# One transfer for the last tile of values, and three pieces of wo instead of four, in a decode attention kernel

## The chip, the cores and the metric

The kernel runs on one core of a Trainium2 chip. The metric is the time of one execution on the device in microseconds (us). Before the change the median of three runs is 190.05 us (189.97 to 190.06).

The core's engines work side by side, each through its own list of instructions in order, and wait for each other by semaphores: TensorE (PE; its weight loads are shown as PEld), VectorE (DVE), ScalarE (ACT), GpSimd (POOL) and SyncE (SP), which here only issues transfers (SPq).

## The reference

One token passes through an attention block with a cache of 4096 positions and through a small two-layer network, and a gate mixes the two. All inputs are bf16, with 32 heads of 128, a model width of 512, and a hidden width of 1376.

```
g = sigmoid((x * gate_w).sum(-1))
q = (x @ wq) per head                       # 32 heads, one query row each
p = softmax(q . k_cache * 128**-0.5)        # over 4096 positions
a = (p . v_cache, heads side by side) @ wo  # (1, 4096) @ (4096, 512)
b = relu(x @ w1 + b1)**2 @ w2 + b2
out = g * a + (1 - g) * b
```

The keys and the values are 32 MB each, wq and wo 4 MB each, w1 and w2 some 2.8 MB together: 78 MB are read for one row of 512 results.

## The kernel before, in words

**Tiles.** The 32 heads are taken four at a time in NQ = 8 tiles. A tile of keys, or of values, is 128 partitions of 32 KB (4 MB): 32 partitions for each head, 128 positions in each partition. Three buffers hold keys (Kt) and two hold values (Vt). The last two tiles of values go into key buffers that have come free (`VT(i)`).

**Order on the engines.** For each tile GpSimd multiplies a part of the keys with the query (L312), VectorE another part (L671) and adds both up (L686, L680), while TensorE transposes the rest (L424) and multiplies it (L438). Then come the maximum (L448, L452), the exponentials on ScalarE (L358), and the sum over the values on TensorE, `pv` (L469): 32 matmuls for a tile, one for each group of four positions, that run in turn in four column strips of the array (the target rows `r = 32 * (y % 4)` of pO). A copy brings pO to pvf, and `extract` (L478, eight matmuls) puts the tile's heads into place in pX.

**The transfers.** SP issues all large loads in one queue, in an order written out by hand (L276 to L293): keys and values in turn, each as soon as its buffer is free, then wo into the first value buffer. The last value tile goes in two transfers (L273, L274): VG = 24 of its 32 groups, then the other eight, each with a semaphore of its own (`s_vl[1]`, `s_vl[2]`). wo, 32 rows of 128 KB (one row per head, 128 partitions by 512 columns), goes in four pieces, whose bounds stand in `TS` (L292).

**The tail on TensorE**, from L590 on: the last but one tile's values and extraction, four fillers (`busy(4)`, L568: matmuls of 512 columns whose result nobody reads), `den()` (the denominators, L485), the last values in two calls of `pv`, three fillers, `extract`, two fillers, `regroup` (L536, which turns the 32 heads' results into columns), three fillers, and then the rows of wo, piece by piece. VectorE lies between these steps: L730 copies pO, L733 divides, L735 copies the regrouped columns.

**Rows of wo.** `attn_rows(c)` waits for piece c. The first WW = 20 rows take one matmul of 512 columns each into pO (L546), in the four strips in turn. The others take four matmuls of 128 columns each, straight into the result in pX (L552). When row 19 is done, VectorE copies pO (L737), and `wide_rows` (L561, eight instructions) adds the copy into pX. After the last row VectorE adds the network's part (L740), and SP sends the result out (L295).

In the kernel before, piece 0 holds rows 0 to 15 and is followed by four fillers; piece 1 holds rows 16 to 23, so the end of the wide rows and the beginning of the narrow ones; before piece 2 (rows 24 to 29) stand two fillers, `wide_rows` and one filler; piece 3 holds rows 30 and 31.

Of the kernel before, what the change touches and what calls it, by code (L numbers as in the profile page):

```python
# [5 lines left out]
def bass_gated_mix__gqa_block_cached__dense_activation_squared_relu__decode_kernel(  # L6
# [22 lines left out]
    NQ = NH // 4  # L29
# [29 lines left out]
    NG = NB // 4  # L59
# [7 lines left out]
    BIG = 3.0e38  # L67


    TS = [0, 16, 24, 30, 32]  # L70
    NW = len(TS) - 1
    WW = 20

    VG = 24


    k_p = A_k_cache.rearrange("a h (q b) d -> (a h q) (b d)", b=NB)
    v_p = A_v_cache.rearrange("a h (q b) d -> (a h q) (b d)", b=NB)
# [7 lines left out]
    with ctx:  # L86
# [6 lines left out]
        def sem(name):  # L93
            return ctx.enter_context(nc.semaphore(name))
# [73 lines left out]
        def VT(i):  # L168
            return Vt[:, i % NV, :] if i < NQ - 2 else Kt[:, (i - 1) % NK, :]
# [21 lines left out]
        s_bb = sem("s_bb")  # L191
        s_k = [sem(f"s_k{i}") for i in range(NK)]
        s_v = [sem(f"s_v{i}") for i in range(NV)]
        s_vl = [sem(f"s_vl{i}") for i in range(3)]
        s_id = sem("s_id")
        s_ho = sem("s_ho")
        s_xc = sem("s_xc")
# [46 lines left out]
        def on(engine):  # L244
            return lambda part: part(engine)

        @on(nc.sync)
        def _(eng):
            def load_k(i):
                if i >= NK:  # L250
                    eng.wait_ge(s_t, CB[i - NK + 1])
                    eng.wait_ge(s_mu, XP * (i - NK + 1))
                    eng.wait_ge(s_pm, GP * (i - NK + 1))
                if i == 2:
                    eng.wait_ge(s_ml, 1)
                eng.dma_start(Kt[:, i % NK, :], k_p[i * 128:(i + 1) * 128, :]).then_inc(s_k[i % NK], 16)

            def load_v(i):
                if i == 1:
                    eng.wait_ge(s_qr, NQ)  # L260
                    eng.wait_ge(s_h, 2)
                if i < NQ - 2:
                    if i >= NV:
                        eng.wait_ge(s_pv, i - NV + 1)
                    eng.dma_start(VT(i), v_p[i * 128:(i + 1) * 128, :]).then_inc(s_v[i % NV], 16)
                    return
                eng.wait_ge(s_t, CB[i])
                eng.wait_ge(s_mu, XP * i)
                eng.wait_ge(s_pm, GP * i)  # L269
                if i == NQ - 2:  # L270
                    eng.dma_start(VT(i), v_p[i * 128:(i + 1) * 128, :]).then_inc(s_vl[0], 16)
                else:
                    for u, a, b in ((1, 0, VG * 512), (2, VG * 512, NG * 512)):  # L273
                        eng.dma_start(VT(i)[:, a:b], v_p[i * 128:(i + 1) * 128, a:b]).then_inc(s_vl[u], 16)  # L274

            load_k(0)  # L276
            eng.dma_start(w1_sb, w1_v).then_inc(s_w1, 16)
            eng.dma_start(w2a, w2_v).then_inc(s_w2, 16)
            eng.dma_start(w2b, B_w2[F0:F1, :]).then_inc(s_w2, 16)
            for r in range(4):  # L280
                eng.dma_start(WX[r:QX:4, :], w2_x[r:QX:4, :]).then_inc(s_w2, 16)
            load_k(1)
            load_v(0)
            load_k(2)
            for i in range(NQ):
                if i >= 1:
                    load_v(i)
                if i + LAG < NQ:
                    load_k(i + LAG)
            eng.wait_ge(s_pv, NQ - 3)  # L290
            for c in range(NW):
                eng.dma_start(WO[:, TS[c] * DM:TS[c + 1] * DM], wo_v[:, TS[c] * DM:TS[c + 1] * DM])\  # L292
                   .then_inc(s_wo[c], 16)  # L293
            eng.wait_ge(s_fin, 1)
            eng.dma_start(out[0, 0, :].rearrange("(j p) -> j p", p=128), b2w[0:128:32, :]).then_inc(s_out, 16)  # L295
            eng.wait_ge(s_out, 16)
# [89 lines left out]
        def _(eng):  # L386
# [69 lines left out]
            def pv(i, a, b):  # L456
                if a == 0:
                    eng.wait_ge(s_e, 4 * (i + 1))
                    if i < NQ - 2:
                        eng.wait_ge(s_v[i % NV], 16 * (i // NV + 1))  # L460
                    else:
                        eng.wait_ge(s_vl[i - (NQ - 2)], 16)
                    if i >= 1:
                        eng.wait_ge(s_pc, i)
                if a == VG and i == NQ - 1:
                    eng.wait_ge(s_vl[2], 16)
                for y in range(a, b):
                    r = 32 * (y % 4)
                    mm = eng.matmul(pO[r:r + 16, :], E[:, i % NE, 4 * y:4 * y + 4, :],  # L469
                                    VT(i)[:, y * 512:(y + 1) * 512], start=(y < 4), stop=(y >= NG - 4))  # L470
                if b == NG:
                    mm.then_inc(s_pv, 1)
# [9 lines left out]
            def den():  # L482
                eng.wait_ge(s_nm, NQ)
                eng.wait_ge(s_e, 4 * NQ)
                eng.matmul(DEN, RS[:, :], onec[:, :], start=True, stop=True).then_inc(s_den, 1)  # L485
# [55 lines left out]
            def attn_rows(c):  # L541
                eng.wait_ge(s_wo[c], 16)
                for t in range(TS[c], TS[c + 1]):
                    r = 32 * (t % 4)
                    if t < WW:
                        mm = eng.matmul(pO[r:r + 1, :], o2[:, t:t + 1], wo_sb[:, t, :], start=(t < 4),  # L546
                                        stop=(t >= WW - 4), skip_group_check=True)
                        if t == WW - 1:
                            mm.then_inc(s_ww, 1)
                        continue  # L550
                    for j in range(4):
                        mm = eng.matmul(acc[32 * j:32 * j + 1, :], o2[:, t:t + 1],  # L552
                                        wo_sb[:, t, j * 128:(j + 1) * 128], start=False,
                                        stop=(t == 31), skip_group_check=True)
                if c == NW - 1:
                    mm.then_inc(s_acc, 1)

            def wide_rows():
                eng.wait_ge(s_wc, 1)
                for j in range(4):  # L560
                    eng.matmul(acc[32 * j:32 * j + 1, :], pick[0:112, 0, 28:29], pvf[:, j * 128:(j + 1) * 128],  # L561
                               start=False, stop=False, skip_group_check=True)
# [3 lines left out]
            def busy(n):  # L566
                for u in range(n):
                    eng.matmul(T[0][:, :], ident[:, :], kT[:, 0, 0:512], start=True, stop=True,  # L568
                               skip_group_check=True)

            for i in range(NQ):
                for c in range(NC[i]):
                    transposes(i, c)
                    if c >= 2:
                        scores(i, c - 2)
                scores(i, NC[i] - 2)
                scores(i, NC[i] - 1)
                if i == 0:
                    mlp_h()
                    mlp_c()  # L580
                    mlp_out()
                if i == 1:
                    mlp_cols()
                if i >= 1:
                    max_rows(i - 1)
                if i >= 3:
                    extract(i - 3)
                if i >= 2:
                    pv(i - 2, 0, NG // 2)
                if i >= 1:  # L590
                    max_cols(i - 1)
                if i >= 2:
                    pv(i - 2, NG // 2, NG)
            extract(NQ - 3)
            pv(NQ - 2, 0, NG)
            max_rows(NQ - 1)
            max_cols(NQ - 1)
            extract(NQ - 2)
            busy(4)
            den()  # L600
            pv(NQ - 1, 0, VG)
            pv(NQ - 1, VG, NG)
            busy(3)
            extract(NQ - 1)
            busy(2)
            regroup()
            busy(3)
            for c in range(NW):
                if c == NW - 2:
                    busy(2)  # L610
                    wide_rows()
                    busy(1)
                attn_rows(c)
                if c == 0:
                    busy(4)

        @on(nc.vector)
        def _(eng):
# [150 lines left out]
```

## Time and profile before

| what | value |
|---|---|
| median of the runs | 190.05 us (189.97 to 190.06) |
| the profiled execution's own time | 190.16 us |
| its span, first to last instruction | 188.8 us |
| mean granted TensorE clock | 0.702 |
| busy: VectorE | 152.5 us (81%) |
| busy: GpSimd | 137.8 us (73%) |
| busy: TensorE matmuls | 106.8 us (57%) |
| busy: ScalarE | 69.4 us (37%) |
| SP's transfers, share of 16 DMA engines' span | 97.2% |
| read from memory | 78.32 MB, 415 GB/s over the span |

The profile shows one execution. An engine's busy time is the sum of its instructions; matmuls overlap in a pipeline and the ends shown are modelled, so the time from one start to the next tells the pace of a series better than their lengths. The granted clock is the share of full speed at which TensorE was allowed to run. An issue of a transfer is the moment at which SP puts it in the queue; its landing is when the last byte's semaphore arrives. The chain of waits goes back from the last instruction, at each step to what released it.

### The profile page before, as it was taken

To read this page: it belongs to the slowest core of one execution; us is meant where nothing else is said; L and a number is where in the kernel's file an instruction comes from. 1 tells how busy PE (TensorE), PEld (TensorE's weight loads), DVE (VectorE), ACT (ScalarE), POOL (GpSimd) and SP (SyncE) were. 2 spreads that over 40 slices of the span, in tenths; PEclk is the share of its full clock that TensorE was granted. 3 is DMA by queue.
4 is the path that set the end of the run, shared out by engine and by line. 5 is a ranking of instruction groups with operands and counts; after the bars stand their busy time and mean duration, and the time that the engine had idled before them with its cause. 6 is when DMAs were issued, how large, how long until landed. Compare 5 with 4: busy or idle time off the path is not lost. (4 is left out here: it accounts for less than half of the span.)

```text
span 188.8 us, 2574 instructions
## 1 busy us (share of the span) xinstructions
PE 106.8 (57%) x1060; PEld 63.0 (33%) x1060; DVE 152.5 (81%) x125; ACT 69.4 (37%) x169; POOL 137.8 (73%) x38
## 2 busy tenths in 40 slices
PE   1139877478102839148506480758184739468985
PEld 0013253337102616133403170418141723224422
DVE  4112569999996999999999999999999999991112
ACT  2103475228220819403920572056305551506000
POOL 1000199989995999979998999899899989940000
PEclk9999999855555756657955876555855556755899
DMA  6999999999999999999999999999999999999992
GB/s 222 445 444 444 388 436 444 437 437 423 422 444 437 423 418 427 437 430 430 434 430 430 430 430 427 437 430 423 437 427 430 430 430 437 427 417 399 437 396 90
DMA packets 3560, 78.47 MB, mean 416 GB/s; under 512 B 439, under 2 KB 457, under 8 KB 734
## 3 DMA queue, kind: packets, MB, share of 16 engines
q1 hardware_dynamic: 3536, 78.32, 97.2%
q8 instruction: 8, 0.13, 0.3%
q14 instruction: 2, 0.02, 0.0%
q10 hardware_dynamic: 14, 0.01, 0.0%
HBM read 78.32 MB, written 0.00 MB: 415 GB/s over the span
## 5 line engine op out<-in xcount | busy, mean ns | idle before, releaser
L312 POOL TENSOR_TENSOR pg<-Kt,qb 128x2176 f32<-128x2176 bf16 x32 | 137.1, 4316 | 28.9 <-DMA Kt<-in_A_k_cache_dram 24.1
L686 DVE TENSOR_REDUCE Sb<-pg 128x17 f32<-128x2176 f32 x32 | 77.0, 2406 | 1.7 <-POOL pg L312 1.6
L341 ACT ACTIVATE kT<-T 128x1024 bf16<-128x1024 bf16 x32 | 30.8, 1030 | 16.0 <-PE T L424 15.9
L424 PE MATMUL T<-ident,Kt 128*128 128x128 bf16 x256 | 25.5, 280 | 17.4 <-DMA Kt<-in_A_k_cache_dram 17.4
L671 DVE TENSOR_TENSOR pr<-Kt,pQ 128x1792 f32<-128x1792 bf16 x16 | 32.2, 2010 | 2.3 <-DMA Kt<-in_A_k_cache_dram 1.5
L680 DVE TENSOR_REDUCE Sb<-pr 128x14 f32<-128x1792 f32 x16 | 32.1, 2004 | 0.0
L424 PEld LDWEIGHTS T<-ident,Kt 128*128 128x128 bf16 x256 | 22.2, 130 | 22.0 <-DMA Kt<-in_A_k_cache_dram 21.2
L469 PE MATMUL pO<-Vt,E 128*16 128x512 bf16 x192 | 21.7, 542 | 0.0
L351 ACT ACTIVATE nM<-pM 128x4 f32<-128x4 f32 x8 | 1.4, 173 | 49.7 <-PE pM L452 49.7
L358 ACT ACTIVATE E<-Sb,nM 32x128 bf16<-32x128 f32 x32 | 18.6, 583 | 0.9
L438 PE MATMUL pS<-qc,kT 128*128 128x4 bf16 x256 | 11.7, 168 | 10.4 <-ACT kT L341 10.1
L478 PE MATMUL pX<-pvf,pick 112*32 112x128 f32 x64 | 14.5, 401 | 2.4 <-ACT pvf L364 2.4
L448 PE MATMUL pM<-identf,mp 128*1 128x128 f32 x8 | 2.9, 359 | 21.3 <-DVE mp L693 21.3
L438 PEld LDWEIGHTS pS<-qc,kT 128*128 128x128 bf16 x256 | 10.0, 102 | 12.6 <-ACT kT L341 12.6
L409 PE MATMUL T<-Vt,kT 128*128 128x512 bf16 x32 | 10.7, 485 | 3.3 <-DMA Vt<-in_A_wq_dram 3.3
L478 PEld LDWEIGHTS pX<-pvf,pick 112*32 112x32 f32 x64 | 9.4, 159 | 6.2 <-ACT pvf L364 2.9
L333 ACT ACTIVATE qb<-T 32x128 bf16<-32x128 f32 x20 | 5.4, 268 | 10.4 <-PE T L409 10.1
L452 PE MATMUL pM<-gm,onesf 1*128 1x4 f32 x16 | 4.1, 322 | 8.8 <-DVE gm L697 8.8
L658 DVE CAST qb<-T 32x128 bf16<-32x128 f32 x12 | 3.4, 286 | 6.6 <-PE T L409 6.3
L469 PEld LDWEIGHTS pO<-Vt,E 128*16 128x16 bf16 x192 | 6.4, 103 | 6.0 <-issue 3.8
L448 PEld LDWEIGHTS pM<-identf,mp 128*1 128x1 f32 x8 | 0.6, 79 | 23.1 <-DVE mp L693 22.7
L358 ACT ACTIVATION_READ_ACCUMULATOR E<-Sb,nM 32x1 f32 x32 | 8.1, 254 | 0.0
(76 smaller groups left out, 72.4 us busy)
## 6 DMA issues: line engine op xcount, KB each, us to landing
Kt<-in_A_k_cache_dram SPq DMA_DIRECT2D x8, 4096.0 KB, 31.1
Vt<-in_A_v_cache_dram SPq DMA_DIRECT2D x6, 4096.0 KB, 31.0
Vt<-in_A_wq_dram SPq DMA_DIRECT2D x1, 4096.0 KB, 12.3
Kt<-in_A_v_cache_dram SPq DMA_DIRECT2D x1, 4096.0 KB, 35.2
Kt<-in_A_v_cache_dram SPq DMA_DIRECT2D x1, 3072.0 KB, 24.5
Vt<-in_A_wo_dram SPq DMA_DIRECT2D x1, 2048.0 KB, 31.0
Kt<-in_B_w_dram SPq DMA_DIRECT2D x1, 1376.0 KB, 24.4
Kt<-in_B_w_dram SPq DMA_DIRECT2D x1, 1280.0 KB
```

The source lines that it names most:

```text
L312: eng.tensor_tensor(pg[:, n % 2, 0:g, :], Kt[:, i % NK, k * g * 128:(k + 1) * g * 128] .rearrange("p (b d) -> p b d", b=g), qb[:, i:i + 1, ...
L333: eng.activation(qb[a:b, j, :], T[j % NT][a:b, h * 128:(h + 1) * 128], ACT.Copy)\
L341: eng.activation(kT[:, n % NR, :], T[n % NT][:, :].bitcast(bf16), ACT.Copy).then_inc(s_ev, 1)
L358: eng.activation(E[a:b, j % NE, :, h], Sb[a:b, j % NS, :], ACT.Exp, bias=nM[a:b, 4 * j + h:4 * j + h + 1], scale=SCALE, accum_out=RS[a:b, ...
L409: mm = eng.matmul(T[j % NT][:, :], xb[:, t, :], wq_sb[:, t, j * 512:(j + 1) * 512], start=(t == 0), stop=(t == 3))
L424: mm = eng.transpose(T[n % NT][:, :].bitcast(bf16)[:, y * 128:(y + 1) * 128], Kt[:, i % NK, w * 128:(w + 1) * 128], ident[:, :])
L438: mm = eng.matmul(S[:, c * TC + y, :], kT[:, n % NR, y * 128:(y + 1) * 128], qc[:, 4 * i:4 * i + 4], start=True, stop=True)
L469: mm = eng.matmul(pO[r:r + 16, :], E[:, i % NE, 4 * y:4 * y + 4, :], VT(i)[:, y * 512:(y + 1) * 512], start=(y < 4), stop=(y >= NG - 4))
L478: mm = eng.matmul(O, pick[0:112, b, 28 - 4 * i:60 - 4 * i], pvf[:, b * 128:(b + 1) * 128], start=False, stop=(i == NQ - 1 and b == 3), ski ...
L671: eng.tensor_tensor(pr[:, 0:x, :], Kt[:, i % NK, a * 128:(a + x) * 128] .rearrange("p (b d) -> p b d", b=x), PQ[:, i % 4:i % 4 + 1, :].bro ...
L680: eng.tensor_reduce(Sb[:, i % NS, a:a + x], pr[:, 0:x, :], AX.X, ALU.add).then_inc(s_sd, 1)
L686: eng.tensor_reduce(Sb[:, i % NS, k * g:(k + 1) * g], pg[:, n % 2, 0:g, :], AX.X, ALU.add)\
```

## The change

The last value tile is loaded by one transfer with one semaphore, and its 32 matmuls wait for the whole of it. wo is loaded in three pieces of 20, 10 and 2 rows, so that the first piece holds just the wide rows. `wide_rows` and its fillers move from before the last but one piece to behind the first: three fillers, `wide_rows`, three fillers, instead of four fillers there and two and one around `wide_rows` later.

```diff
-    TS = [0, 16, 24, 30, 32]
+    TS = [0, 20, 30, 32]
     NW = len(TS) - 1
     WW = 20
-
-    VG = 24
...
-        s_vl = [sem(f"s_vl{i}") for i in range(3)]
+        s_vl = [sem(f"s_vl{i}") for i in range(2)]
...
                 eng.wait_ge(s_pm, GP * i)
-                if i == NQ - 2:
-                    eng.dma_start(VT(i), v_p[i * 128:(i + 1) * 128, :]).then_inc(s_vl[0], 16)
-                else:
-                    for u, a, b in ((1, 0, VG * 512), (2, VG * 512, NG * 512)):
-                        eng.dma_start(VT(i)[:, a:b], v_p[i * 128:(i + 1) * 128, a:b]).then_inc(s_vl[u], 16)
+                eng.dma_start(VT(i), v_p[i * 128:(i + 1) * 128, :]).then_inc(s_vl[i - (NQ - 2)], 16)
...
                     if i >= 1:
                         eng.wait_ge(s_pc, i)
-                if a == VG and i == NQ - 1:
-                    eng.wait_ge(s_vl[2], 16)
...
             den()
-            pv(NQ - 1, 0, VG)
-            pv(NQ - 1, VG, NG)
+            pv(NQ - 1, 0, NG)
             busy(3)
...
             for c in range(NW):
-                if c == NW - 2:
-                    busy(2)
-                    wide_rows()
-                    busy(1)
                 attn_rows(c)
                 if c == 0:
-                    busy(4)
+                    busy(3)
+                    wide_rows()
+                    busy(3)
```

## The prediction

> **What bounds the kernel now.** I read four views, from the end backwards. First the chain of waits (columns: start us, length us, what). It goes back over one transfer of wo that was issued at 151.86 and landed at 186.46; only 2.3 us of the span lie behind that landing.
>
> ```profile
> 149.96 0.42 SPq L274
> ...
> 151.86 34.59 DMA Vt<-in_A_wo_dram
> 186.44 0.04 issue
> 186.49 0.31 PE pX L552 x8
> 186.80 0.02 issue
> 186.82 0.29 DVE b2w L740
> ```
>
> Second, the DMA issues (size, us from issue to landing). With the start times of the issues in the timeline (149.59, 149.96, then 150.44, 150.91, 151.38, 151.86) they give the landings: the last value tile at 174.09 (24 of its 32 groups) and 176.56 (the other 8), wo at 181.44, 183.91, 185.78 and 186.46. The page moves about 430 GB/s in nearly every slice: the queue never runs dry, so the last byte comes when it does whatever the engines do.
>
> ```profile
> Kt<-in_A_v_cache_dram SPq DMA_DIRECT2D x1, 3072.0 KB, 24.5
> Vt<-in_A_wo_dram SPq DMA_DIRECT2D x1, 2048.0 KB, 31.0
> Kt<-in_A_v_cache_dram SPq DMA_DIRECT2D x1, 1024.0 KB, 26.6
> Vt<-in_A_wo_dram SPq DMA_DIRECT2D x1, 1024.0 KB, 33.0
> Vt<-in_A_wo_dram SPq DMA_DIRECT2D x1, 768.0 KB, 34.4
> Vt<-in_A_wo_dram SPq DMA_DIRECT2D x1, 256.0 KB, 34.6
> ```
>
> Third, TensorE's timeline of the tail (start us, length us, then the work).
>
> ```profile
> 166.87 3.59 PE L469 MATMUL pO<-Kt,E 128*16 128x512 bf16 x32 [1.80 <-issue]
> ...
> 171.90 1.92 PE L478 MATMUL pX<-pvf,pick 112*32 112x128 f32 x8
> 173.75 1.89 PE L568 MATMUL T<-kT,ident 128*128 128x512 bf16 x4
> ...
> 175.69 2.06 PE L469 MATMUL pO<-Kt,E 128*16 128x512 bf16 x29
> 177.69 0.82 PE L568 MATMUL T<-kT,ident 128*128 128x512 bf16 x3
> ...
> 181.52 1.03 PE L546 MATMUL pO<-Vt,o 128*1 128x512 bf16 x16
> ...
> 184.20 0.40 PE L552 MATMUL pX<-Vt,o 128*1 128x128 bf16 x16
> ...
> 185.86 0.91 PE L552 MATMUL pX<-Vt,o 128*1 128x128 bf16 x32
> ```
>
> The reader is to see two things. The values' matmuls of the last tile (L469) start at 175.58, 1 us before their tile is complete, because the first piece is already there; the second piece's wait costs nothing. And the same 32 matmuls took 3.59 us at 166.87 and 2.2 us here. The fourth view says why: stretches of 3.41 us with TensorE's busy us, instructions and the granted clock.
>
> ```profile
> 107.81:111.22 3.41, 2.67 (x28) 0.50 0.98 423
> 165.83:169.25 3.42, 2.38 (x24) 0.50 1.01 431
> 172.66:176.07 3.41, 3.41 (x19) 0.50 1.00 420
> 176.07:179.49 3.42, 3.37 (x43) 1.00 1.00 426
> ```
>
> The clock is half or full and changes on a grid of 3.41 us. A stretch with 2.67 us of dense matmuls (107.81) is followed by full clock (1.00 in the row for 111.22 to 114.63), one with 2.38 (165.83) is not. Before the last values the stretch is full, and the clock doubles at 176.07.
>
> **The change, part by part.** *Issues.* SP issues one value transfer for two and three of wo for four: two fewer of 0.42 and 0.43 us, so SP comes to its last wait (34.8 us long) 0.85 us earlier. No issue is nearer than 24 us to its landing, so the queue's depth hides this: 0. Without that depth it would be a gain of 0.85.
>
> *The stream.* Tile 6 of the values, unsplit, landed at 131.60 + 35.2 = 166.80, the tile before it at 125.88 + 31.2 = 157.08: 9.72 us for 4 MB. The split tile took 176.56 - 166.80 = 9.76 and wo in four pieces 9.90. So a cut costs 0.04 to 0.06. With one cut fewer in each the last tile lands at 176.52, and wo's pieces at 182.63 (20 rows: 4.88 us for 16 by the row for 2048 KB, plus half of 2.47), 185.70 and 186.36: 0.10 us gained. Bounds: 0 and 0.2 (twice the two differences).
>
> *The wait in front of the last values.* They can start only when the whole tile is there: 176.52 plus the 0.07 us that lie between landing and matmul (166.80 to 166.87; 181.44 to 181.52), so 176.59 instead of 175.58. Behind them on TensorE stand three fillers (L568), the extraction, the regrouping and all of wo; VectorE's copy L730 waits for them. What they then cost depends on the clock. At full clock: four run side by side, one set per 0.213 us (the 16 of L546 took 1.03, of which the last one's own latency is 0.38), so eight sets are 1.87, end 178.46. At half clock: 3.59 by the row at 166.87, end 180.18. Before they ended at 177.75.
>
> *Which clock.* Ahead of the wait TensorE has eight extraction matmuls from 171.90 (0.213 us apart, so to 173.60), four fillers from 173.75 (0.427 apart, to 175.46) and two tiny ones for the denominator, then nothing until 176.59. On the grid of this profile the stretch 172.66 to 176.07 would hold 0.94 + 1.71 = 2.65 us of matmuls, which is near the 2.67 that was enough. If the grid lay 0.5 us later, it would hold 0.44 + 1.71 = 2.15, less than the 2.38 that was not; from there to 1.7 us later, no more than 2.3, since the pause of 1.13 us is inside. If it lay earlier, the extraction fills it (0.5 earlier: 1.44 + 1.71 = 3.15) until about 1.5 us earlier. The grid's edges fall together with no instruction or landing of this kernel, so I take every position of the grid as equally likely from one execution to the next. With the cautious price (2.65 and more needed) the clock comes up in time in 1.5 of 3.41 us, and late in 1.9. In the kernel before, the values go on through the pause and fill the stretch at almost every position; this is the cover that is removed.
>
> [...]
>
> *Late clock, the sum.* Values end at 180.18. From their end to the end of the fillers ahead of wo took 181.56 - 177.75 = 3.81 at full clock, and the grid's next edge (179.7 to 181.2) restores it before the extraction at 181.0: 183.99. All 20 rows of the first piece are there (182.63): 1.03 + 0.21 = 1.24, end 185.23. Copy L737 0.05 + 0.69: 185.97. The eight wide_rows 0.05 later take 0.33 to the next instruction (185.17 to 185.50): 186.35. Three fillers at 0.213: 186.99. Then 40 narrow matmuls of rows 20 to 29, four per 0.055 us (the 24 at 185.86): 0.55, then the last eight, 0.055 + 0.22: 187.81, against 186.80 now. So +1.0 us: 190.16 + 1.0 in the profiled execution's terms, which is 0.11 above the median of the runs shown; on that median 190.05 + 1.0 = 191.05.
>
> *Other edits.* The three fillers in front of wide_rows run while VectorE copies; one filler fewer in all (6 for 7) is 0.21, inside the late sum already. The second wait's removal is 0.
>
> **The rivals.** *In time.* The clock is full at 176.59. Values end at 178.46, rows of wo can start at 178.46 + 3.81 = 182.27, before the landing at 182.63: 0.36 us to spare. Then rows to 183.94, copy to 184.68, wide_rows to 185.06, fillers to 185.70, 40 narrow matmuls from 185.78 to their last start at 186.28, and the last piece's eight from 186.39: end 186.70, 0.10 earlier than now. Time 189.95, not slower. For it: 2.65 beside 2.67 at this grid, a stream without gaps. Against it: it needs some 2.4 to 2.65 us of matmuls in the stretch that ends between 174.5 and 176.3, and half of the positions do not have them.
>
> *Later still.* The grid's next stretch does not fill either (some 1.5 us early, where it holds 0.78 of fillers and 1.5 of values), and extraction and regrouping run at half clock too: 0.86 more for the extraction (1.92 for 1.06) and some 0.5 for fillers and regrouping: about 192.3. Only a strip of positions gives it.
>
> *Issue pace.* 48 matmuls with 48 weight loads stand in one run where the trace has at most 24. Lower bound of the pace 0.014 us each (four per 0.055), upper 0.041 (62 matmuls between 183.99 and 186.55, pauses included). I take 0.014, the same instruction; at 0.041 the last run takes 1.97 for 0.66, which on the in-time sum is some +0.9: 190.85. Nothing in the 24 shows a slowing.
>
> *Faster.* Two transfers fewer would have to give 0.4 us or more. The rows say 0.2 at most; 189.6 if they are wrong by that much.
>
> **How the numbers follow.** Late clock 0.47, in time 0.41, later still 0.05, issue pace 0.03, faster 0.04. The likeliest gives 191.05; its own range is 190.7 (the clock returns while the values still run) to 191.4. The full range, 189.8 to 191.5, holds both main cases and the pace. A measurement of this kernel tells about 0.2% (0.38 us) from no change. Slower by more: late, later and most of the pace, 0.54. Within: in time and the rest, 0.42. Faster: 0.04.
>
> **What would show it.** Late clock: in the changed profile the 32 values start near 176.6 with a granted clock of 0.5, last some 3.5 us, and the first rows of wo start after their landing, waiting for the regrouping and not for the DMA. In time: 2 us for the values, rows at 182.7 waiting for the DMA. The runs' times should scatter, or fall in two groups 1.1 us apart, if the grid moves; three runs of the kernel before lie within 0.09. The stream's step is wrong if the last wo piece lands later than 186.46. The whole is wrong if the values do not wait for their tile, or if the end again follows the last landing by 0.3 us with the values at half clock.

## The result and the profile after

The changed kernel took 190.85 us (median of seven executions, 189.86 to 190.99), the kernel before 190.05 (189.93 to 190.16) beside it. The ratio of the means is 1.003, with a 95% interval of 1.0016 to 1.0044. The seven do not lie round their median. Two are at 189.86 and 190.08, five between 190.83 and 190.99, nothing lies between. The profiled execution (190.87 us, span 189.5) is one of the late five.

Its issues of wo (size, us from issue to landing):

```profile
Vt<-in_A_wo_dram SPq DMA_DIRECT2D x1, 2560.0 KB, 32.8
...
Vt<-in_A_wo_dram SPq DMA_DIRECT2D x1, 1280.0 KB, 35.4
Vt<-in_A_wo_dram SPq DMA_DIRECT2D x1, 256.0 KB, 35.5
```

They were issued at 149.60, 150.07 and 150.54, so they landed at 182.40, 185.47 and 186.04; the last value tile, issued at 149.22, took 27.1 and landed at 176.32. From the landing of the value tile before it (166.52) to the last byte are 19.52 us, where the kernel before has 186.46 - 166.80 = 19.66. The transfers are not what became later: the stream gained 0.14 (a landing is known to 0.1).

The chain of waits no longer goes back over a transfer of wo. From the denominator on (start us, us, what) it runs through TensorE and the copies of VectorE:

```profile
174.09 0.20 PE pM L477 x2
174.29 2.08 issue
176.37 3.06 PE pO L461 x32
179.42 1.24 PE T L560 x3
180.66 1.00 PE pX L470 x8
...
182.76 0.82 PE T L560 x3
183.58 1.21 PE pO L538 x20
184.82 0.70 DVE pvf L726
```

The 2.08 us called issue are the wait for the value tile, which landed 0.05 us before its 32 matmuls began (L461, before L469). They took 3.06 us, against 2.2 before and 1.90 at full clock (the changed kernel's second profile, below). Row 0 of wo (L538) starts at 183.51, 1.1 us after its landing, so no row of wo waits for its transfer any more. Why they took 3.06 is seen in the same execution's stretches of the clock's grid (3.41 us each; TensorE's busy us, instructions, and the granted clock, 0.50 or 1.00 in every stretch of this profile):

```profile
166.72:170.13 3.41, 3.41 (x32) 0.50 1.00 432
170.13:173.55 3.42, 2.57 (x18) 1.00 1.02 441
173.55:176.96 3.41, 0.79 (x14) 1.00 0.90 386
176.96:180.37 3.41, 3.41 (x30) 0.50 1.03 441
```

The clock was already full at 170.13, brought up by the values of the tile before. The pause leaves 0.79 us of work in the stretch 173.55 to 176.96, and with its end the clock falls to half, 0.59 us after the last values have begun.

### The profile page after: what moved, and what is told of

It is laid out like the page before. It is cut to its first block, busy times and chain, and to the rows that moved or that the text cites. A ratio compares the mean times of both kernels' runs of the same rounds, so it can differ in the third digit from the quotient of the medians.

```text
span 189.5 us, 2568 instructions
## 1 busy us (share of the span) xinstructions
PE 110.2 (58%) x1057; PEld 64.8 (34%) x1059; DVE 152.6 (81%) x125; ACT 69.4 (37%) x169; POOL 137.8 (73%) x38
## 5 line engine op out<-in xcount | busy, mean ns | idle before, releaser
L418 PE MATMUL T<-ident,Kt 128*128 128x128 bf16 x256 | 27.2, 292 | 17.0 <-DMA Kt<-in_A_k_cache_dram 17.0
L418 PEld LDWEIGHTS T<-ident,Kt 128*128 128x128 bf16 x256 | 23.6, 135 | 21.6 <-DMA Kt<-in_A_k_cache_dram 19.9
L461 PE MATMUL pO<-Vt,E 128*16 128x512 bf16 x192 | 23.5, 583 | 0.0
L470 PE MATMUL pX<-pvf,pick 112*32 112x128 f32 x64 | 13.6, 385 | 1.6 <-ACT pvf L358 1.6
L403 PE MATMUL T<-Vt,kT 128*128 128x512 bf16 x32 | 9.3, 438 | 3.3 <-DMA Vt<-in_A_wq_dram 3.3
L461 PEld LDWEIGHTS pO<-Vt,E 128*16 128x16 bf16 x192 | 6.6, 108 | 6.8 <-issue 5.2
L461 PE MATMUL pO<-Kt,E 128*16 128x512 bf16 x64 | 6.6, 589 | 3.8 <-issue 3.8
```

The lines of the kernel that those rows point to most:

```text
L403: mm = eng.matmul(T[j % NT][:, :], xb[:, t, :], wq_sb[:, t, j * 512:(j + 1) * 512], start=(t == 0), stop=(t == 3))
L418: mm = eng.transpose(T[n % NT][:, :].bitcast(bf16)[:, y * 128:(y + 1) * 128], Kt[:, i % NK, w * 128:(w + 1) * 128], ident[:, :])
L470: mm = eng.matmul(O, pick[0:112, b, 28 - 4 * i:60 - 4 * i], pvf[:, b * 128:(b + 1) * 128], start=False, stop=(i == NQ - 1 and b == 3), ski ...
```

## The experiments

A late execution is here one above 190.6; none of the 88 executions of the kernel before in its four series reached that (highest 190.50, medians of the series 190.03 to 190.10). Counts are used where there are two groups, since a median then jumps from one group to the other.

| kernel | executions | late | median us | lowest to highest |
|---|---|---|---|---|
| changed, first series | 7 | 5 | 190.85 | 189.86 to 190.99 |
| changed, second series | 12 | 4 | 190.01 | 189.79 to 191.15 |
| tile split, wo in three pieces | 11 | 2 | 190.03 | 189.92 to 191.56 |
| tile whole, wo in four pieces | 12 | 7 | 191.21 | 189.85 to 191.57 |
| changed, no fillers ahead | 4 | 4 | 192.06 | 191.84 to 192.23 |
| changed, eight ahead | 12 | 7 | 190.87 | 189.85 to 191.10 |
| changed, twelve ahead | 12 | 0 | 190.07 | 189.72 to 190.51 |
| changed, four ahead and four behind | 12 | 3 | 190.04 | 189.80 to 191.17 |
| before, no fillers ahead | 11 | 0 | 190.10 | 189.96 to 190.42 |
| split, three pieces, ten fillers ahead of wo | 11 | 0 | 190.06 | 189.77 to 190.39 |

**The two halves of the change, one by one.** First only the value tile is split again:

```diff
-                eng.dma_start(VT(i), v_p[i * 128:(i + 1) * 128, :]).then_inc(s_vl[i - (NQ - 2)], 16)
+                if i == NQ - 2:
+                    eng.dma_start(VT(i), v_p[i * 128:(i + 1) * 128, :]).then_inc(s_vl[0], 16)
+                else:
+                    for u, a, b in ((1, 0, VG * 512), (2, VG * 512, NG * 512)):
+                        eng.dma_start(VT(i)[:, a:b], v_p[i * 128:(i + 1) * 128, a:b]).then_inc(s_vl[u], 16)
...
+                if a == VG and i == NQ - 1:
+                    eng.wait_ge(s_vl[2], 16)
...
-            pv(NQ - 1, 0, NG)
+            pv(NQ - 1, 0, VG)
+            pv(NQ - 1, VG, NG)
```

> The last value tile in two transfers again, wo in three pieces as in the changed kernel. Wait theory (the values' wait for their whole tile, with a pause in which the clock is lost, costs the 0.8 us): the values start near 175.6 or earlier and end by 177.8, the end is set by the last wo landing: every execution 189.9 to 190.0. Pieces theory (the 20-row piece and the wide rows behind it cost the time): 190.8 as the changed kernel. A mixed theory: with values done early and 20 rows landing only at 182.5, TensorE pauses some 2 us before wo, and at some positions of the clock's grid the rows run at half clock: executions scatter between 189.9 and 191.2.

Nine of eleven lie at 189.92 to 190.27, two at 191.41 and 191.56. So the pieces theory falls, the wait theory holds for most, and the mixed theory would have the other two. Two of eleven against nine of the changed kernel's nineteen is not proof by itself; the other half of the change, below, gives the stronger count. In the profiled execution (189.97) TensorE's timeline shows both waits that are now there:

```profile
174.26 1.47 PE L469 MATMUL pO<-Kt,E 128*16 128x512 bf16 x24
176.50 0.61 PE L469 MATMUL pO<-Kt,E 128*16 128x512 bf16 x8 [0.77 <-DMA Kt<-in_A_v_cache_dram]
...
182.61 1.25 PE L546 MATMUL pO<-Vt,o 128*1 128x512 bf16 x20 [1.70 <-DMA Vt<-in_A_wo_dram]
```

The first 24 groups cut the pause to 0.77 us. But with the values done early the second pause ahead of the 20 rows is 1.70 us; in the kernel before there was none there.

The other half alone, the kernel before with its last value tile in one transfer:

```diff
-                if i == NQ - 2:
-                    eng.dma_start(VT(i), v_p[i * 128:(i + 1) * 128, :]).then_inc(s_vl[0], 16)
-                else:
-                    for u, a, b in ((1, 0, VG * 512), (2, VG * 512, NG * 512)):
-                        eng.dma_start(VT(i)[:, a:b], v_p[i * 128:(i + 1) * 128, a:b]).then_inc(s_vl[u], 16)
+                eng.dma_start(VT(i), v_p[i * 128:(i + 1) * 128, :]).then_inc(s_vl[i - (NQ - 2)], 16)
...
-                if a == VG and i == NQ - 1:
-                    eng.wait_ge(s_vl[2], 16)
...
-            pv(NQ - 1, 0, VG)
-            pv(NQ - 1, VG, NG)
+            pv(NQ - 1, 0, NG)
```

> The last value tile in one transfer, wo in four pieces as before. Wait theory: the values start near 176.5, at half clock in more than half of the executions; rows of wo start at 183.3 to 184.0 instead of 181.5, two groups of times, near 190.0 and near 190.8. Pieces theory: 190.05 with no scatter, as the kernel before.

Two groups as expected, five at 189.85 to 190.21 and seven at 191.12 to 191.57; the late one is some 0.6 us later than expected, and later than the changed kernel's. Why is open, since no late execution of this kernel was profiled. But seven of twelve, against none of 88 of the kernel before, show that the whole transfer alone brings the late group. The profiled execution was in time (190.21): its values start at 176.75, as late as in the changed kernel, and run at full clock.

```profile
175.48 0.27 PE L479 MATMUL pM<-onec,RS 128*32 128x1 f32 x2
176.75 1.90 PE L463 MATMUL pO<-Kt,E 128*16 128x512 bf16 x32 [0.99 <-issue]
```

So the late start by itself costs nothing that the stream does not hide. That the whole transfer costs where the clock goes with it is shown on the changed kernel, above.

**How many fillers.** In the changed kernel the four fillers ahead of the denominator became none, twelve, and then eight:

```diff
             extract(NQ - 2)
-            busy(4)
+            busy(12)
             den()
```

> The changed kernel without the four fillers ahead of the denominator (their result is read by nobody). Clock theory (what decides is how much of a 3.41 us stretch ahead of the values TensorE works): fewer executions with full clock at the values, median 190.9 to 191.5, none or nearly none at 189.9. Rival (the start of the values at 176.4 alone decides, the clock is incidental): unchanged, 190.85 median with the same two groups, or a little faster since TensorE has less in front of the values.

> The changed kernel with twelve fillers instead of four ahead of the denominator, so that TensorE works through the pause: 2.6 us at full clock, 5.1 at half. Clock theory: the clock is full while the values run at nearly every position of the grid; the values may start up to 1 us later, yet the end is set by the last wo landing, 189.8 to 190.0 in every execution, below both kernels. Rival (the late start alone decides, the clock is incidental): the values start later still, so 190.9 to 191.6.

> The changed kernel with eight fillers instead of four ahead of the denominator: 1.7 us at full clock, 3.4 at half, so to 177.1 at the latest, 0.4 us earlier than with twelve. Clock theory: no or few executions in the slow group, and the upper part of the spread seen with twelve (to 190.5, the fillers themselves in the way) is gone: 189.75 to 190.1, median 189.9. Rival (any filler in front of the values costs what it takes): 190.4 and more.

None: all four executions late, 1.1 us beyond the changed kernel's late group. Here the clock never came up ahead of the values:

```profile
171.92:175.33 3.41, 1.90 (x10) 0.50 0.91 393
175.33:178.75 3.42, 2.15 (x24) 0.50 1.05 449
178.75:182.16 3.41, 3.41 (x23) 0.50 0.93 393
```

Their 32 matmuls took the whole 3.59 us. Twelve: none of twelve is late, although in the profiled execution the fillers ran from 173.48 to 177.5 and the values began at 177.47, 0.9 us later than their tile allows; that one took 190.49 and is in the upper part of the spread, where the fillers themselves are in the way: the rows of wo start at 183.16 without waiting for their transfer. The rival, that the late start alone decides, falls with it. How twelve help is shown by the count alone. By the pace of its fillers (4.05 us for the twelve) the clock of the profiled execution rose at about 176.1, a position that the forecast held safe with four fillers too.

Eight: wrong. I expected the late group to go and it has 7 of 12. So it had to be asked which way the clock is lost.

**The pause, not the fillers' count.** Two theories were left for the late executions. Rise: the clock had not come up because the stretch ahead of the values was not full. Fall: it was up, and the pause took it away. I moved four of the eight into the pause:

```diff
             busy(4)
             den()
+            busy(4)
             pv(NQ - 1, 0, NG)
```

> The changed kernel with four more fillers, as in the run with eight, but behind the denominator instead of ahead of it, so in the pause itself. Theory fall (the clock is already full from tile 6's values on, the fillers ahead of the denominator are over before ScalarE's exponentials, which the denominator awaits at 174.1, and the pause of 2.1 us behind it empties the stretch and takes the clock away): these four shorten that pause to 1.2 us, and the slow group, 7 of 12 with eight ahead, goes: 0 to 2 of 12 above 190.6, the others 189.8 to 190.4. Theory rise (the clock had not come up because the stretch ahead of the values was not full): the count of fillers decides and not their place, so a slow group as with eight ahead.

Three of twelve are late (7 of 12 with all eight ahead). That is fewer, but more than the 0 to 2 that theory fall allowed, and with twelve executions not proof by itself. The execution that was profiled was in time, so why those three were late is open. Two more profiles of the kernel with all eight ahead show more.

> One more profile of the kernel with eight fillers ahead. If it falls into the slow group (190.8 to 191.1), theory fall expects full clock from about 170 on, an idle TensorE from 174.3 to the values, and the clock back to half within the values; theory rise expects half clock throughout from 162 to behind the start of the values. In the fast group both expect full clock at the values and the end 0.3 us behind the last landing.

> As the look before it, for another position of the clock's grid: in the slow group theory fall expects a clock that falls within the values after a pause of some 2 us, theory rise one that has not come up at all.

Both fell into the late group (191.10 and 191.03), and both show the fall, as the changed kernel's late profile does. The first:

```profile
172.53 1.68 PE L560 MATMUL T<-kT,ident 128*128 128x512 bf16 x7 [0.16 <-issue]
174.16 0.20 PE L477 MATMUL pM<-onec,RS 128*32 128x1 f32 x2
176.58 3.46 PE L461 MATMUL pO<-Kt,E 128*16 128x512 bf16 x32 [2.22 <-issue]
```

```profile
169.54:172.95 3.41, 2.59 (x25) 1.00 0.98 423
172.95:176.37 3.42, 1.41 (x8) 1.00 0.99 423
176.37:179.78 3.41, 3.20 (x32) 0.50 0.97 414
```

At full clock the eight fillers are over just when the denominator can start, since that waits for the exponentials on ScalarE until about 174.1. What was added ahead of it fills time in which TensorE would wait anyway; the pause behind it stays 2.2 us. It leaves 1.41 us of work in its stretch, and the clock falls at 176.37, 0.2 us before the values begin. The second has the same picture: a pause of 2.21 us, and values of 3.11 us from 176.54. Worked out from that length (3.06 with a fall 0.59 us in, in the changed kernel's late execution), the clock falls at about 177.1, behind a stretch with some 1.2 us of work.

**What covered this before.** The kernel before without its four fillers:

> The kernel before without its four fillers ahead of the denominator (nobody reads their result). Clock theory: the last values can start at 174.2 on their first piece and TensorE is never idle long, so what fills the stretch is the values themselves; the clock comes up during them or behind them, and no execution is slow: 190.0 to 190.3. Rival (the four fillers alone set the clock for the tail, the split tile matters little): slow as the changed kernel without fillers, 191 to 192.

None of eleven is late. In the profiled execution (190.08) the clock was at half as in the run without fillers above, and the values took the same 3.59 us. But they ran from 174.61 to 178.2, not from 176.60 to 180.2:

```profile
174.61 3.59 PE L469 MATMUL pO<-Kt,E 128*16 128x512 bf16 x32
```

The first piece of the tile, not the fillers, covers the tail.

**The second pause.** The kernel with the tile split and three pieces got ten fillers in place of three between the regrouping and wo:

```diff
             regroup()
-            busy(3)
+            busy(10)
             for c in range(NW):
```

> The last value tile in two transfers, wo in three pieces, and ten fillers instead of three between the regrouping and the rows of wo (2.1 us at full clock, from 180.1 to 182.2; the 20 rows land at 182.5). Clock theory: the two executions near 191.5 seen with three fillers come from a second pause, the one ahead of the 20 rows; with it filled all executions are 189.8 to 190.1, median 189.95. Rival (those two had another cause): some 2 in 11 still above 191; or the fillers are in the way and all are later by 0.2 or more.

None of eleven is late, against two of eleven, which fits the second pause as their cause and is too few to show it; no late execution of that kernel was profiled. The median, 190.06, is no better than the kernel before beside it (190.09; ratio 0.9997, interval 0.9989 to 1.0006).

**The changed kernel again.**

> The changed kernel once more, for more executions and a second profile with another position of the clock's grid. Clock theory: two groups, 189.85 to 190.15 and 190.8 to 191.1, the slower with 50 to 70 of 100; if the profiled execution is of the fast group its values run at full clock, some 1.9 us, and the rows of wo wait for their transfer. Rival (the two groups come from the transfers): the last wo landing is later in the slow group.

Four of twelve were late, fewer than the 50 to 70 in 100 expected, with 5 of 7 in the first series: together 9 of 19. By itself this series would have been no change (median 190.01; ratio of the means 1.001, interval 0.9994 to 1.0025). Over both series the mean is 190.42, 0.3 to 0.4 us above that of the kernel before beside them. The profile is of an execution in time (189.97). The clock came up at 175.10 from a full stretch and stayed up with 2.36 us of work in the next:

```profile
171.69:175.10 3.41, 3.41 (x13) 0.50 1.03 441
175.10:178.51 3.41, 2.36 (x36) 1.00 0.94 402
```

The values ran 1.90 us from 176.57, and the rows of wo waited 0.37 us for their transfer. From the landing of tile 6 (166.76) to the last byte (186.28) are 19.52 us, as in the late execution: the two groups do not come from the transfers.

## Why the prediction was right, and where not

**The time.** 191.05 was forecast for the likeliest case, with 0.47 for it and 0.41 for the clock in time. The first series' median is in the late group; over both series 9 of 19 are late and 10 in time. That the median on record lies near 191.05 is therefore luck: the second series gave 190.01. What the forecast had right is the two groups, 1.1 us apart in its sums and 0.97 measured: the late nine average 190.93 and the other ten 189.96.

**The issues and the stream.** A cut was taken at 0.04 to 0.06 us, 0.10 for both. Measured is 0.14, in the late execution and in the one in time. Right, a little small.

**The wait.** The values were to start at 176.59; they start at 176.37 to 176.57, 0.05 to 0.11 behind their landing. Right.

**Which clock.** The forecast said that the pause decides by what it leaves in a stretch of the grid, and that the grid's position changes from one execution to the next. The second is shown: edges lie at 176.07 in the profile of before, and at 176.96, 176.37 and 175.10 in others. For the first speak the three late executions that were profiled with fillers ahead (one of the changed kernel, two with eight): in each the clock fell behind a stretch that the pause had emptied. But one step was wrong: I took the clock to be at half ahead of the last values at every position and asked only whether it rises. In all three it had risen at 169.5 to 170.3 with the values of tile 6. Then the fillers take about half as long (four of them 1.04 us at full clock and 1.89 at half in the profile of before), the pause is 2.1 to 2.2 us and not 1.1, and the clock falls. A late clock by not rising was seen only without fillers; whether it also happens in the changed kernel stays open.

The forecast's sorting of the positions came out all the same, over a path that it did not have, and so in part by luck. It called an edge between 174.5 and 176.3 safe. The three late executions have theirs at 176.37 (just beyond), 176.96 and about 177.1. Of the five in time with a whole tile and fillers, whatever their number, one has it at 175.10, and for three the pace of the fillers puts it at about 175.0 (four and four), 175.2 (eight) and 176.1 (twelve). With wo in four pieces it is known only to lie between 175.5, where four fillers end that took the 1.89 us of half clock, and the values at 176.75.

**The late sum.** +1.0 was forecast, the profile has +0.7 (187.49 for 186.80 at the last matmul). The mis-sized term is the values: 3.59 was taken, half clock throughout, and 3.06 measured, since the clock is still full for the first 0.59 us. The landing is 0.2 earlier in that execution. Against these, the fillers behind the values still ran partly at half clock, 1.30 for 0.82.

**In time.** The last matmul was forecast to end at 186.70 and ended at 186.60, time 189.95 against 189.97 in the profiled execution.

**Issue pace.** The 48 narrow matmuls in one run took 0.84 us, the 0.055 per four that was taken and no slowing. That rival is out, and so are the two others: nothing near 192.3 in the changed kernel, nothing near 189.6.

## What to carry to other kernels

When transfers set the end, an engine off that path can still take it over if a wait empties it. Here a pause of 2.08 us on TensorE was followed by half clock and by values of 3.06 us for 1.90, and the late executions average 0.97 us more: look at what the pause does to TensorE's clock, not only at its length. Look where fillers fall: ahead of another wait they first fill time that is idle anyway, and eight of them left the pause at 2.2 us. That filling the pause itself does better is not shown, since 3 of 12 were late with four fillers in it and none of 12 with twelve ahead. Where times come in two groups, count the executions in each: three or seven can give either median.

## What the runs showed that I had not expected

Pauses of 2.08 us (the changed kernel) and of 2.21 and 2.22 us (eight fillers ahead) were enough to lose the clock. Behind stretches with 0.79, some 1.2 and 1.41 us of work it fell; behind two with 1.83 and 1.68 it stayed full (the split kernel, where the three fillers at 184.99, behind the last of these lines, took the 0.82 us of full clock):

```profile
173.23:176.65 3.42, 1.83 (x31) 1.00 1.11 467
176.65:180.06 3.41, 3.07 (x25) 1.00 0.95 408
180.06:183.47 3.41, 1.68 (x20) 1.00 0.97 405
```

The busy time of a stretch is not the whole measure, though, neither here nor in the forecast. In the kernel before, a stretch at full clock with 2.25 us (63.43 to 66.84) was followed by half clock (0.50). And one that was busy throughout (39.51 to 42.92, with the network's one-row matmuls and transposes of keys) did not bring the clock up: it stayed at 0.50 in the next. Which matmuls count for the clock, and how much, no run here separates.
